# Which queue begins the attention's stores: SyncE or ScalarE

## The chip, the cores and the metric

The kernel runs on one core of a Trainium2 chip. A core has a TensorE (PE, matmuls; PEld is its weight loads), a VectorE (DVE), a ScalarE (ACT), a GpSimd (POOL) and a SyncE (SP), each with an instruction queue of its own that is worked off in order, and they wait for one another through semaphores. Transfers between DRAM and the core's memory are begun by an instruction in the queue of SP or of ACT and are carried out by 16 DMA engines. The metric is device time in microseconds (us) of one execution; lower is better.

## What is computed

A linear recurrence with a complex, input-dependent gate, per batch and head, and a gated feed-forward block behind it. Sizes: batch 4, heads 8, sequence 768, head dimension 48, model width 384, inner width 1024.

```python
for t in range(S):                      # S_re, S_im: 48 x 48 per batch and head
    new_re = ar * S_re - ai * S_im      # ar, ai: the gate at t, its size capped at 0.999
    new_im = ar * S_im + ai * S_re
    S_re, S_im = new_re + k[t] v[t]^T, new_im
    y[t] = q[t] S_re
x = y as (batch, seq, 384)
h = gelu(x @ w_in);  u, v = halves of h
v_n = layernorm(v) * g_ln
v_s[t] = sum over s of w_sg[t, s] * v_n[s] + b_sg[t]
out = x + (u * v_s) @ w_out
```

## The kernel before

The recurrence is worked as attention in chunks of 128 positions: 4 batches of 6 chunks, numbered 0 to 23. The gates' logarithms and phases are summed along the sequence, `q` and `k` are turned by them into `Q` and `K` (two rows of 48 per head), and for each chunk the masked products `am` and the state `S` of the chunk before are multiplied with `V` and `Q` into `py`, in PSUM. From batch 1 on, the turned `q` and `k` go through DRAM (`rq`, `rk`) and come back as `Q` and `K` in the layout that the matmuls want.

The step at issue is the end of `attend(g)`, chunk by chunk. `py` is copied into the tile `yp` (128 partitions x 512 floats) by ACT, or, where the order carries a mark, by DVE. `yp` has one buffer. Then two DMAs, one for the even and one for the odd heads, store it into the DRAM buffer `xd[b][j]`, which holds the attention's result of 256 positions, two chunks. That makes 24 chunks x 2 = 48 stores of 96 KB. The feed-forward part begins with `load_x`, which reads `xd[b][j]` back, transposed by the way it was laid out, from SP's queue; it is read a second time for the residual. `normal` computes the normed half, `expand` the other, `spatial` the mix over positions and the output product.

The order of all work is written out by hand. Each step of the kernel is a Python generator, and the string `ORDER` names which one goes on next: `a2` is the attention of chunk 2, `z` loads or makes `K` and `Q`, `g`, `e`, `p`, `s` and `t` are the gates' functions, `w` prepares weights, `n`, `x` and `y` are the feed-forward parts, `v` and `l` are loads, `h` and `k` check the inputs' range. `a0:2` takes two steps, a prime moves a copy from ACT to DVE (or an elementwise operation to POOL or DVE). The program order on each engine is the order in which the tokens emit instructions for it. The copy into `yp` is one step of `attend`, and the two stores are the next. In some chunks the two follow each other directly, as for chunk 15 (`a15:2`); mostly other tokens stand between them. Chunk 2's copy is the last `a2` of line 39 and its stores the `a2` of line 40:

```python
n0:5 a3 z4 g5 z4:6 z5 m4 a2 e3 v4 m4 e4 a4 v5 a3 p4 z4 e4' e4 e4' p4 z5 a4:3 z5 e3 z5' a4 p4 s4:3 a3 n1 n0 e4 g5 n0
```

Between the two, `z4` has ACT copy three tiles of `K` and `Q`, and `g5` and others run on it. On ACT's queue the stores' place is therefore behind those. Chunk 5's stores stand behind a copy of `dec` (`e4`), chunk 11's behind `vh` (`n4` and `n3`), chunk 12's behind the logarithm of a gate unit (`g10`), chunk 16's ahead of `x7`. SP's queue holds nearly all other DMAs in the same order: the loads of gates, `q`, `k`, `v`, weights and `x`, the round trip through `rk` and `rq`, and the output's stores. Each of its instructions waits for what it reads, for the buffer that it writes, and for the DMA that used its semaphore before. Only the last three stores of the output are begun by ACT.

Of the kernel before, what the change touches and what calls it, by code (L numbers as in the profile page):

```python
# [75 lines left out]
def tile_kernel(ctx: ExitStack, tc: tile.TileContext, t_q, t_k, t_re, t_im, u_q, u_k, u_re, u_im, v, q, k, f_re, f_im,  # L76
                w_in, g_ln, w_sg, b_sg, w_out, out):
    nc = tc.nc


    B, S, H, D = v.shape
# [112 lines left out]
    def ew():  # L194

        return nc.gpsimd if alt[0] == 1 else nc.vector

    def evac(out, in_):
        if alt[0]:
            nc.vector.tensor_copy(out, in_)  # L200
        else:
            nc.scalar.copy(out, in_)  # L202
# [101 lines left out]
    def fea(n):  # L304
        return units[n][0] > 0
# [247 lines left out]
    def attend(g):  # L553
        n, i = at_chunk[g]
        b, c = divmod(g, NCH)
        u = U[n]
        V = vbuf[g % 2]
        K, Q = (lambda h, nm=nm: u[nm, i, h // 4][:, h % 4, :] for nm in "KQ")
        last = c == NCH - 1
        if not last and not fea(n):  # L560
            kh = lambda h: u["k0", i][:, h].rearrange("p a d -> p (a d)")
        elif not last:
            kh = lambda h: kt_[:, h]
            kt_ = ap_.tile([P, H, 2 * D], F32, tag="kt", name="kt", bufs=2)
            for g2 in range(2):
                pk = pst.tile([P, 4, 2 * D], F32, tag="t", name="pk")
                for hh in range(4):
                    nc.tensor.transpose(pk[:, hh, :], K(4 * g2 + hh), ident[0:2 * D, 0:2 * D])  # L568
                yield
                evac(kt_[:, 4 * g2:4 * g2 + 4, :], pk)  # L570
                yield
        ams = []
        for g2 in range(2):
            pa = pst.tile([P, 4, P], F32, tag="t", name="pa")
            for hh in range(4):
                h = 4 * g2 + hh
                nc.tensor.matmul(pa[:, hh, :], K(h), Q(h), start=True, stop=True)  # L577
            yield
            am = ap_.tile([P, 4, P], F32, tag="am", name="am", bufs=2)
            nc.vector.tensor_tensor(out=am, in0=pa, in1=mask.unsqueeze(1).broadcast_to([P, 4, P]), op=ALU.mult)  # L580
            ams.append(am)
            yield
        Sb = run.get(("S", g - 1))
        if not last:
            ps = pst.tile([2 * D, H, D], F32, tag="t", name="ps")
            for h in range(H):
                nc.tensor.matmul(ps[:, h, :], kh(h), V[:, h * D:(h + 1) * D], start=True, stop=True)  # L587
            yield
            Sn = ap_.tile([2 * D, H, D], F32, tag="S", name="S", bufs=2)
            if c == 0:  # L590
                by = u["dec"][:, i, :].unsqueeze(2).broadcast_to([2 * D, H, D])
                nc.vector.tensor_tensor(out=Sn, in0=ps, in1=by, op=ALU.mult)
            else:
                nc.vector.tensor_tensor(out=Sn, in0=ps, in1=Sb, op=ALU.add)
                yield
                by = u["dec"][:, i, :].unsqueeze(2).broadcast_to([2 * D, H, D])
                ew().tensor_tensor(out=Sn, in0=Sn, in1=by, op=ALU.mult)
            run["S", g] = Sn
            yield
        py = pst.tile([P, NP, P], F32, tag="t", name="py")  # L600
        for p_ in range(NP):
            for e in range(2):
                h = 2 * p_ + e
                nc.tensor.matmul(py[64 * e:64 * e + 64, p_, :], V[:, h * D:h * D + 64], ams[h // 4][:, h % 4, :],  # L604
                                 start=True, stop=c == 0)
            if c > 0:
                for e in range(2):
                    h = 2 * p_ + e
                    nc.tensor.matmul(py[64 * e:64 * e + D, p_, :], Sb[:, h, :], Q(h),  # L609
                                     start=False, stop=True)  # L610
        yield
        yp = ap_.tile([P, NP, P], F32, tag="yp", name="yp", bufs=1)
        evac(yp, py)
        yield
        j, r = divmod(c, UC)
        dst = xd[b][j].rearrange("(p e d) t -> e d p t", e=2, d=D)[:, :, :, r * P:(r + 1) * P]
        for e in range(2):
            nc.sync.dma_start(out=dst[e], in_=yp[64 * e:64 * e + D])
        yield


# [266 lines left out]
    for g in range(B * NCH):  # L888
        chains.update({f"v{g}": load_v(g), f"r{g}": rotate(g), f"z{g}": heads(g), f"a{g}": attend(g)})
# [59 lines left out]
```

## Time and profile before

| | us |
|---|---|
| median of 2 runs | 462.36 (460.3 and 464.41) |
| the profiled execution | 457.97 |
| its span, first to last instruction | 456.3 |
| PE idle within the span | 35.6 |
| SP: waits of the stores for a copy by ACT, 10 of them | 25.2 |
| SP: waits of `x` loads for the stores, 6 of them | 12.5 |
| ACT: waits of a `yp` copy for the stores before it, 2 of them | 7.4 |

How to read the profile's lines. A line of a timeline gives the start in us, the length in us, engine, source line, operation, what is written and read, shapes, count, and in brackets the idle time of the engine just before it with what ended it. SPq and ACTq are instructions of a queue that keep its engine's datapath idle: issues of DMAs and waits. A line of the table of windows gives the stretch in us, its length, busy time of PE, PEld, DVE, ACT and POOL with the number of instructions, the TensorE clock granted, the DMA engines' share and the GB/s moved. A view of one tile lists its instructions with minimum, median and maximum length in ns. In the chain of waits a row is a start, a length and what the end of the program waited for in that stretch; a DMA there is its way from the issue to the landing. The page's rows of DMA queues give packets, MB and share.

### The profile page before, as it was taken

Reading aid. Unit: us, or ns where it says so; the run is one execution under the profiler, and the core shown is the slowest. Engines: PE = TensorE matmul, PEld = TensorE weight load, DVE = VectorE, ACT = ScalarE, POOL = GpSimd, SP = SyncE. Lnnn points to the kernel's source line nnn. Section 1 sums busy time; section 2 is a strip of 40 time slices with the busy share of each in tenths; the row PEclk is TensorE's granted clock in tenths of the full one; section 3 lists DMA queues with packets and bytes.
Section 4 is the critical chain, followed back from the end, with each engine's and each line's share of the span. In section 5 each row is a group of like instructions: output and inputs, shape, how many; then the busy total and the mean of one; then the engine's idle time right before and its main releaser. Section 6 shows DMA issues by size and latency. Waiting matters only on the chain.

```text
span 456.3 us, 9462 instructions
## 1 busy us (share of the span) xinstructions
PE 420.7 (92%) x3658; PEld 388.5 (85%) x3658; DVE 372.1 (82%) x646; ACT 284.9 (62%) x383; POOL 170.6 (37%) x208
## 2 busy tenths in 40 slices
PE   1568898899999999999999999999999999999994
PEld 0255697788999999999999989998999989989994
DVE  4999999899899989998886897679797637875643
ACT  6899999698969999958568546675540312321000
POOL 7036223726446385143233528632314303423000
PEclk9999999999999999999999999999999999999999
DMA  7688675667766787876857696695688684625321
GB/s 224 228 246 253 209 214 130 207 184 244 210 185 212 254 256 232 252 234 203 227 161 270 170 349 203 206 290 193 185 241 265 209 245 145 178 71 185 106 70 42
DMA packets 67710, 93.40 MB, mean 205 GB/s; under 512 B 9540, under 2 KB 52550, under 8 KB 67656
## 3 DMA queue, kind: packets, MB, share of 16 engines
q1 hardware_dynamic: 67224, 92.32, 66.6%
q8 instruction: 30, 0.49, 0.5%
q10 hardware_dynamic: 432, 0.39, 0.3%
q14 instruction: 24, 0.20, 0.1%
HBM read 69.09 MB, written 23.60 MB: 203 GB/s over the span
## 4 chain that ended last, share of the span: by engine, by line
PE 60%; DVE 14%; DMA 9%; ACT 7%; POOL 4%; issue 3%; SPq 2%; POOLq 0%; DVEq 0%; ACTq 0%
PE pvs L219 17%; PE pu L219 9%; PE pa L577 8%; PE po L219 7%; PE pv L219 7%; PE ps L587 4%; DMA K<-rk 3%; PE py L604 3%; PE py L609 2%; ACT L188 2%; DMA x<-xd 2%; PE pk L568 2%; DMA xd<-yp 1%; DMA raw<-in_moe_w_in_dram 1%; DVE im L367 1%
## 5 line engine op out<-in xcount | busy, mean ns | idle before, releaser
L188 ACT ACT_TABLE_LOAD x67 | 86.0, 1283 | 2.0 <-PEq L934 0.8
L219 PE MATMUL pvs<-wsgh,vh 128*128 128x256 f32 x288 | 82.4, 286 | 0.1
L219 PE MATMUL pvs<-wsgh,vl 128*128 128x256 f32 x288 | 81.1, 282 | 0.4 <-DVE vl L689 0.3
L219 PE MATMUL pvs<-wsgl,vh 128*128 128x256 f32 x288 | 80.9, 281 | 0.0
L577 PE MATMUL pa<-Q,K 96*128 96x128 f32 x384 | 49.9, 279 | 6.0 <-ACT Q L202 3.2
L219 PEld LDWEIGHTS pvs<-wsgh,vh 128*128 128x128 f32 x288 | 54.3, 189 | 0.8 <-issue 0.4
L219 PEld LDWEIGHTS pvs<-wsgh,vl 128*128 128x128 f32 x288 | 54.3, 188 | 0.8 <-DVE vl L689 0.8
L219 PEld LDWEIGHTS pvs<-wsgl,vh 128*128 128x128 f32 x288 | 54.3, 189 | 0.0
L577 PEld LDWEIGHTS pa<-Q,K 96*128 96x128 f32 x384 | 45.9, 192 | 9.7 <-ACT Q L202 4.3
L219 PE MATMUL pu<-xh,winh 128*128 128x256 f32 x144 | 42.6, 296 | 0.2 <-ACT dec L202 0.2
L219 PE MATMUL po<-gh,wouth 128*128 128x256 f32 x144 | 41.7, 290 | 0.6 <-DVE gh L211 0.6
L219 PE MATMUL po<-gl,wouth 128*128 128x256 f32 x144 | 40.8, 283 | 1.3 <-POOL gl L214 1.0
L219 PE MATMUL pu<-xh,winl 128*128 128x256 f32 x144 | 40.6, 282 | 0.0
L219 PE MATMUL pu<-xl,winh 128*128 128x256 f32 x144 | 40.5, 282 | 0.0
L219 PE MATMUL po<-gh,woutl 128*128 128x256 f32 x144 | 40.5, 282 | 0.0
L604 PE MATMUL py<-am,vbuf 128*64 128x128 f32 x384 | 36.5, 278 | 0.8 <-DVE am L580 0.8
L580 DVE TENSOR_TENSOR am<-pa,mask 128x512 f32<-128x512 f32 x48 | 31.8, 678 | 5.5 <-PE pa L577 5.4
L609 PE MATMUL py<-Q,S 96*48 96x128 f32 x320 | 31.2, 272 | 0.0
L189 ACT ACTIVATE vr<-pv 128x512 f32<-128x512 f32 x24 | 14.2, 598 | 24.6 <-PE pv L219 16.8
L219 PE MATMUL pv<-winh,xh 128*128 128x512 f32 x72 | 29.2, 406 | 0.0
L219 PEld LDWEIGHTS po<-gl,wouth 128*128 128x128 f32 x144 | 27.2, 189 | 1.9 <-POOL gl L214 1.2
L219 PEld LDWEIGHTS po<-gh,wouth 128*128 128x128 f32 x144 | 27.1, 188 | 1.5 <-DVE gh L211 0.8
(287 smaller groups left out, 1144.7 us busy)
## 6 DMA issues: line engine op xcount, KB each, us to landing
x<-xd SPq DMA_DIRECT2D x24, 384.0 KB, 4.7
K<-rk SPq DMA_DIRECT2D x18, 384.0 KB, 5.7
Q<-rq SPq DMA_DIRECT2D x18, 384.0 KB, 5.0
vbuf<-in_v_dram SPq DMA_DIRECT2D x24, 192.0 KB, 3.7
xd<-yp SPq DMA_DIRECT2D x48, 96.0 KB, 3.5
gr<-in_f_re_dram SPq DMA_DIRECT2D x12, 384.0 KB, 3.6
gr<-in_f_im_dram SPq DMA_DIRECT2D x12, 384.0 KB, 3.4
re<-in_u_re_dram SPq DMA_DIRECT2D x9, 384.0 KB, 5.4
```

What stands on the lines that cost most here:

```text
L188: nc.scalar.preload_act_table_set(SETS[t])
L189: nc.scalar.activation(out, in_, func, scale=scale, **kw)
L219: nc.tensor.matmul(o, w(i), x(i), start=(i == 0 and j == 0), stop=(i == n - 1 and j == 2))
L367: ew().tensor_mul(im, im, e)
L568: nc.tensor.transpose(pk[:, hh, :], K(4 * g2 + hh), ident[0:2 * D, 0:2 * D])
L577: nc.tensor.matmul(pa[:, hh, :], K(h), Q(h), start=True, stop=True)
L580: nc.vector.tensor_tensor(out=am, in0=pa, in1=mask.unsqueeze(1).broadcast_to([P, 4, P]), op=ALU.mult)
L587: nc.tensor.matmul(ps[:, h, :], kh(h), V[:, h * D:(h + 1) * D], start=True, stop=True)
L604: nc.tensor.matmul(py[64 * e:64 * e + 64, p_, :], V[:, h * D:h * D + 64], ams[h // 4][:, h % 4, :], start=True, stop=c == 0)
L609: nc.tensor.matmul(py[64 * e:64 * e + D, p_, :], Sb[:, h, :], Q(h), start=False, stop=True)
```

## The change

The two stores of each chunk are begun from ACT's queue instead of SP's. They keep their place in the hand-written order, so they stand on ACT behind whatever ACT instructions come before the stores' token. Data, shapes and the `yp` buffer stay as they were.

```diff
         j, r = divmod(c, UC)
         dst = xd[b][j].rearrange("(p e d) t -> e d p t", e=2, d=D)[:, :, :, r * P:(r + 1) * P]
         for e in range(2):
-            nc.sync.dma_start(out=dst[e], in_=yp[64 * e:64 * e + D])
+            nc.scalar.dma_start(out=dst[e], in_=yp[64 * e:64 * e + D])
         yield
```

## The prediction

> **What bounds the kernel now.** I read the page first, then the table of windows, then the view of the tile `yp`, then the timelines of SyncE's queue (SP), ScalarE (ACT) and TensorE (PE) where PE stands idle, and last the chain of waits. The page:
>
> ```profile
> span 456.3 us, 9462 instructions
> PE 420.7 (92%) x3658; PEld 388.5 (85%) x3658; DVE 372.1 (82%) x646; ACT 284.9 (62%) x383; POOL 170.6 (37%) x208
> q10 hardware_dynamic: 432, 0.39, 0.3%
> ```
>
> PE is busy for 420.7 us of 456.3. A gain can only come out of the 35.6 us in which it isn't, most of them before the first store starts at 41.2 us. A loss comes wherever PE's next operand is late. ACT's 62% is a mean over unlike stages, so the table of windows (PE, PEld, DVE, ACT, POOL):
>
> ```profile
> 30.00:60.00 30.00, 25.37 (x198) 19.50 (x198) 29.19 (x52) 28.63 (x45) 11.48 (x9) 1.00 0.80 238
> 75.00:90.00 15.00, 11.83 (x116) 10.51 (x113) 13.88 (x24) 11.26 (x19) 9.80 (x8) 1.00 0.71 202
> 90.00:105.00 15.00, 13.84 (x117) 12.36 (x118) 13.22 (x21) 14.88 (x19) 5.00 (x5) 1.00 0.75 216
> 125.00:218.00 93.00, 93.00 (x854) 88.91 (x853) 87.03 (x131) 79.03 (x97) 43.45 (x41) 1.00 0.75 229
> ```
>
> Up to 105 us ACT is nearly full and PE has holes; from 125 to 218 PE has none, ACT is at 85%. The stores, from the view of `yp`, and the only DMAs that ACT issues today:
>
> ```profile
> L618 SPq DMA_DIRECT2D xd<-yp x48: 303/434/1279, 41.2 to 390.1; - x48
> L200 DVE COPY yp<-py x5: 676/681/692, 120.0 to 327.2; 128x512 f32<-128x512 f32 x5
> DMA to landing us min/median/max: 1.9/3.5/6.4
> L753 ACTq DMA_DIRECT2D out_dram<-x x3: 338/381/912, 449.7 to 451.9; - x3
> ```
>
> So 24 pairs, each two issues of 0.434 us in the median, landing 3.5 us after the issue. `yp` has one buffer: the next copy waits until the pair before it has landed. PE's four places that the change can reach:
>
> ```profile
> 78.97 1.16 PE L577 MATMUL pa<-Q,K 96*128 96x128 f32 x8 [1.27 <-ACT Q L202]
> 103.17 0.44 PE L568 MATMUL pk<-ident,K 96*128 96x96 f32 x3 [1.13 <-DMA K<-rk]
> 225.74 0.47 PE L568 MATMUL pk<-ident,K 96*128 96x96 f32 x3 [0.51 <-ACT yp L202]
> 373.22 0.47 PE L568 MATMUL pk<-ident,K 96*128 96x96 f32 x3 [1.05 <-DMA K<-rk]
> ```
>
> The brackets hold PE's idle time and what ended it: one copy on ACT, two K loads that stand behind stores on SP, one `yp` copy that waited for a landing. Together they are 3.96 us.
>
> **The change part by part.** Removed: 48 issues from SP, 48 x 0.434 = 20.8 us, and SP's waits for `yp` ahead of them. Added: the same 20.8 us and waits to ACT's queue, at the place of the store's token in the hand-written order, which is often several ACT instructions after the copy's token. Nothing else is reordered, and the bytes are the same. What counts is where each pair stands on ACT against where it stood on SP.
>
> *Chunk 2, about 76 us, the largest term.*
>
> ```profile
> 72.69 0.88 SPq L618 DMA_DIRECT2D xd<-yp  x2
> 77.72 1.57 SPq L618 DMA_DIRECT2D xd<-yp  x2
> 81.22 0.38 SPq L640 DMA_DIRECT2D x<-xd  x1
> 94.81 0.81 SPq L618 DMA_DIRECT2D xd<-yp  x2
> 96.65 0.43 SPq L548 DMA_DIRECT2D K<-rk  x1
> ...
> 75.89 0.59 ACT L202 COPY K<-pk 96x512 f32<-96x512 f32 x1
> 76.37 0.86 ACT L189 ACTIVATE em<-l 128x768 f32<-128x768 f32 x1
> 77.11 0.58 ACT L202 COPY yp<-py 128x512 f32<-128x512 f32 x1
> 78.32 0.59 ACT L202 COPY Q<-pk 96x512 f32<-96x512 f32 x1
> 95.74 1.28 ACT L188 ACT_TABLE_LOAD   x1
> ```
>
> By the order the pair of chunk 2 stands between the `K` copy of 75.89 and the `em` of 76.37. SP issued it at 72.69. On ACT the first issue can begin once the `K` copy is under way, about 75.97, the second at 76.4, and 3.5 us later, at 79.9, it has landed. The `yp` copy of chunk 3, now at 77.11, waits for that: 79.9 - 77.11 = 2.8 us. Behind it on ACT stand the `Q` copy of 78.32, for which PE waits at 78.97 with no slack, and the exponentials of that unit. So 2.8 us on the path. Bounds by the same view's 1.9 and 6.4: 1.2 to 5.7.
>
> *Chunk 5, 95 us, and the K load.* SP stood at the pair of 94.81 until `yp` was copied, and the K load of 96.65, for which PE waits at 103.17, was queued behind it. With the pair gone from SP, K waits only for what it reads and for its buffer, and PE's hole of 1.13 us closes: -1.1 (bounds -1.13 to 0, the latter if `rk`, itself later by the term before, is then what ends last). On ACT the pair comes before the table load of 95.74, behind a short copy that covers little: ACT is later by up to 0.8, in a window where it is busy 14.88 of 15 us. I take 0.4 (0 to 0.8).
>
> *Chunks 9 and 8, 166 to 172 us.*
>
> ```profile
> 166.47 0.94 ACT L189 ACTIVATE inv<-l,cols 128x768 f32<-128x768 f32 x1
> ...
> 169.69 0.59 ACT L202 COPY yp<-py 128x512 f32<-128x512 f32 x1
> 172.04 0.60 ACT L189 ACTIVATE vr<-pv 128x512 f32<-128x512 f32 x1 [0.46 <-PE pv L219]
> ```
>
> Chunk 9's pair stands behind the `inv` of 166.47; its second issue is at 166.95 at the earliest and lands at 170.45, 0.8 after the `yp` copy of 169.69 wants to start. Chunk 8's pair stands directly behind that copy and is bare, 0.87. Less the 0.46 of slack, the `vr` of 172.04 is 1.2 late. PE has other work queued there; I take 0.5 (0 to 1.2).
>
> *Chunk 11, 197 us.*
>
> ```profile
> 192.88 0.80 SPq L618 DMA_DIRECT2D xd<-yp  x2
> 196.86 0.38 SPq L640 DMA_DIRECT2D x<-xd  x1
> 196.66 0.73 ACT L189 ACTIVATE vh<-vr,ny 128x512 fp32r<-128x512 f32 x1
> 201.84 0.84 ACT L189 ACTIVATE xh<-x 128x768 fp32r<-128x768 f32 x1 [1.47 <-PE pu L219]
> ```
>
> The pair comes behind the `vh` of 196.66, and SP's load of `x`, which reads what it stores, goes from 196.86 to about 197.1 + 3.5 = 200.6, with six loads queued behind it. That is 3.7 us on a load whose reader, `xh`, has 1.47 us of idle time ahead of it. I take 0.6 (0 to 2.2).
>
> *Chunk 12, 219 us.*
>
> ```profile
> 218.19 0.99 SPq L618 DMA_DIRECT2D xd<-yp  x2
> 218.62 6.42 DMA xd<-yp
> 219.37 0.94 ACT L189 ACTIVATE l<-l,cols 128x768 f32<-128x768 f32 x1
> 225.10 0.58 ACT L202 COPY yp<-py 128x512 f32<-128x512 f32 x1 [4.80 <-DMA xd<-yp]
> ```
>
> Here the landing itself is on the path: 6.42 us after the issue, behind three loads on the same queue, then the `yp` copy, then PE at 225.74. ACT reaches the pair while it runs the `l` of 219.37, so the second issue goes from 218.62 to 219.8, 1.2 later. If the landing takes as long as now, that is +1.2; if it no longer stands behind the three loads, the hole of 0.51 closes. I take +0.6 (-0.5 to 1.2).
>
> *Chunk 20, 364 us.*
>
> ```profile
> 363.69 0.87 SPq L618 DMA_DIRECT2D xd<-yp  x2
> 365.60 0.48 SPq L548 DMA_DIRECT2D K<-rk  x1
> ```
>
> SP issues from the pair to the K load without a break; take out 0.87 and K goes that much earlier, against a hole of 1.05 us at 373.22. But the stores' bytes travel at the same time all the same: -0.6 (-1.05 to 0).
>
> *The rest.* Chunks 0 and 1 fall in the window where ACT is busy 28.63 of 30 us: +0.4 (0 to 2 x 0.87 = 1.7). The other pairs I cost at nothing: they are covered by the ACT instruction before them or by an idle stretch behind; if that cover is gone, each costs ACT 0.87. Five copies are made by DVE, and there ACT now waits for DVE. The longest such wait is chunk 16's:
>
> ```profile
> 294.86 0.81 SPq L618 DMA_DIRECT2D xd<-yp  x2
> 296.09 0.60 ACT L189 ACTIVATE u__3690<-pu 128x512 f32<-128x512 f32 x1 [2.87 <-PE pu L219]
> ```
>
> By the order its pair stands on ACT ahead of a table load and this gelu. ACT is held from about 292 until 294.86 + 0.87 = 295.7, the table load (1.28) ends at 297.0, and the gelu is 0.9 late. PE wants its buffer only some matmuls later: 0 (0 to 0.9). The program's DMAs also take turns on eight semaphores, and each issue waits for the DMA eight before it; at the pairs' places on ACT that one has landed, but for chunk 15, where ACT has a long idle stretch behind the pair: 0.
>
> The sum: 2.8 - 1.1 + 0.4 + 0.5 + 0.6 + 0.6 - 0.6 + 0.4 = 3.6 us, between -1.5 and 13.8 when all ends are added. The profiled execution took 457.97 us, of which 456.3 are its span; 457.97 + 3.6 = 461.6. It is 4.4 us under the median of the two runs shown, 462.36, and on that scale, on which I predict, it is 466.0.
>
> How long an issue holds ACT is the open price. The row of 77.72 shows a pair of 1.57 us on SP against 0.88 for that of 72.69. [...] No run here shows both queues issuing at once.
>
> **The rivals.**
>
> *ACT becomes the bound.* Nothing in the trace shows a DMA issue beside ACT's own work: the three that it has run at the end, when it is idle. If nothing covers an issue, the pairs up to 105 us, six of them, cost 6 x 0.87 = 5.2 instead of the parts of them counted above, and the six that ACT would issue from 125 to 218 us, at 85% ACT, as much again; with the late landing of chunk 2 and the K load's gain, 5.2 + 5.2 + 2.8 - 1.1 = 12.1 us: 474.5. For it: ACT's 14.88 of 15 us. Against it: PE's work ahead in the 93 us without a hole. It decides if the pairs from 125 on cost more than about 0.4 us of PE each.
>
> *Faster: SP was the queue that hurt.* If a store no longer queues behind loads, chunk 2's pair lands soon enough that the `Q` copy is not late, and the holes at 103.17, 225.74 and 373.22 close: -1.13 - 0.51 - 1.05 = -2.7 us, 459.7. For it: 6.42 us of landing at 218.62 against 1.9 for the fastest. Against it: even 1.9 us lands chunk 2 at 78.3, after 77.11. It decides if ACT starts that pair before about 75.2 us, that is, if its queue runs ahead of its engine. [...]
>
> *The change does nothing that shows.* Every late pair is taken up by PE's work ahead: -0.5 to +0.5, 462.4. Against it: the 78.97 row has no slack.
>
> **How the numbers follow.** Two per cent is 9.2 us, about what a measurement of this kernel can tell from no change. The forecast, +1 to +9 us, gets 0.5; no visible effect 0.14; the faster rival 0.15, nearly all of it within 2%; ACT as the bound 0.21, of which 0.17 is over 2%. Faster by over 2% would need PE to lose 9.2 us of holes where the stores reach 3.96: 0.04. So slower 0.18, same 0.78, faster 0.04. The range goes from the faster rival less 1.7 for the spread of the runs shown, 458, to the end of the ACT rival, 474.
>
> **What would show it.** The line of the stores appears under ACT's queue with 48 issues and no longer under SP's; the second DMA queue goes from 432 packets and 0.39 MB to about 5.1 MB (48 x 96 KB more). PE's wait for the `Q` copy near 79 us grows from 1.27 to about 4 us, with ACT's `yp` copy before it held by a landing. The hole at 103 us is gone or small; the `x` load near 197 us starts 3 to 4 us later. The prediction is wrong if the `yp` copy near 77 us does not wait, if the pairs' issues on ACT take much over 0.43 us each, or if PE shows new holes between 125 and 218 us.

## The result, and the profile after

| | before | after |
|---|---|---|
| median of two runs, us | 462.36 (460.3 to 464.41) | 477.12 (475.3 to 478.94) |
| profiled execution: time and span, us | 457.97 and 456.3 | 475.3 and 473.6 |
| its mean granted clock of TensorE | 0.998 | 0.978 |

The changed kernel takes 1.0339 times as long, with a 95% interval of 1.0277 to 1.0401: slower by 14.8 us. The forecast was 466.0, with a range of 458 to 474, and no difference that can be measured as the likeliest class. Both were wrong.

From the page of the kernel after: the span, the engines' busy times, the granted clock in 40 slices, the two DMA queues (packets, MB, share of the engines) and the chain that ended last, by engine.

```profile
span 473.6 us, 9463 instructions
PE 430.4 (91%) x3658; PEld 396.6 (84%) x3658; DVE 370.6 (78%) x646; ACT 285.2 (60%) x383; POOL 168.4 (36%) x208
PEclk9999999697999999999999999998999999999999
q1 hardware_dynamic: 57240, 87.60, 60.3%
q10 hardware_dynamic: 10416, 5.12, 4.0%
PE 55%; DMA 16%; DVE 15%; ACT 8%; POOL 3%; issue 2%; SPq 0%; ACTq 0%; DVEq 0%; POOLq 0%
```

ACT is busy for 285.2 us, where it was 284.9: the issues did not fill it. PE is busy for 9.7 us longer with the same 3658 instructions, and the row of its clock, all nines before, has dips. So time went in two ways: PE stood idle longer, and behind that it ran slower. The view of the tile `yp`:

```profile
L618 ACTq DMA_DIRECT2D xd<-yp x48: 309/404/1213, 41.2 to 407.4; - x48
  ACT yp L202: 19.8, 4
  DVE yp L200: 4.5, 2
DMA to landing us min/median/max: 1.9/4.6/9.9
```

An issue costs 0.404 us in the median, not more than the 0.434 on SP. But the pairs now land 4.6 us after the issue instead of 3.5, at most 9.9 instead of 6.4, and copies on ACT wait 19.8 us for such landings, those on DVE 4.5. (The trace tells the landing of 24 of the 48 stores before and of 36 after, so the two medians are not of the same stores; the waits are of all copies.)

Where the time is lost shows best against PE's own progress. Take the end of the last matmul into `py` (L604, L609) of the 2nd, 6th, 8th, 12th, 16th, 18th and 22nd chunk in PE's order, and the time from each to the next; in the kernel before these ends lie at 49.79, 93.54, 121.42, 189.24, 252.59, 290.24 and 362.56 us. All of it is worked out from the timelines of the profiled executions:

```
stretch of before, us   0-50   50-94  94-121 121-189 189-253 253-290 290-363 363-end
before                 49.79   43.75   27.87   67.83   63.34   37.65   72.33   93.70
after                  49.63   49.03   34.39   68.09   64.75   37.52   76.80   93.38
after less before      -0.16   +5.28   +6.52   +0.26   +1.41   -0.13   +4.47   -0.32
```

The sum is +17.3, the difference of the spans, and 16.3 of it lies in three stretches. Each has one place, and the timelines of the kernel after show it (start, duration, engine, line, operation; in brackets the idle time ahead and what ended it).

```profile
75.91 0.46 ACTq L618 DMA_DIRECT2D xd<-yp  x1
80.44 0.59 ACT L202 COPY yp<-py 128x512 f32<-128x512 f32 x1 [3.18 <-DMA xd<-yp]
81.67 0.57 ACT L202 COPY Q<-pk 96x512 f32<-96x512 f32 x1
82.29 1.01 PE L577 MATMUL pa<-Q,K 96*128 96x128 f32 x3 [4.67 <-ACT Q L202]
...
96.18 0.33 SPq L548 DMA_DIRECT2D K<-rk  x1
96.56 0.75 SPq L329 DMA_DIRECT2D k<-in_u_k_dram  x1
98.87 0.33 SPq L548 DMA_DIRECT2D Q<-rq  x1
99.29 0.38 SPq L548 DMA_DIRECT2D K<-rk  x1
99.92 0.81 ACTq L618 DMA_DIRECT2D xd<-yp  x2
110.23 0.59 ACT L202 COPY yp<-py 128x512 f32<-128x512 f32 x1 [6.76 <-DMA xd<-yp]
111.36 0.58 PE L219 MATMUL pu<-xh,winh 128*128 128x256 f32 x1 [5.28 <-ACT vr L189]
```

First place: chunk 2's pair, issued at 75.91, lands just before 80.44; chunk 3's copy has waited 3.18 us for it, `Q` stands behind the copy, and PE has stood for 4.67 us. Second place: chunk 5's pair of 99.92 lands at about 110.2, the next copy has held ACT for 6.76 us, and PE has stood for 5.28. In the kernel before, SP issued `k`, `Q`, `K` and `q` behind that pair, within 2.4 us (its timeline; the `K` of 96.65 stands between the last two); now four such loads go in the 4 us ahead of it.

```profile
95.67 0.46 SPq L329 DMA_DIRECT2D k<-in_u_k_dram  x1
96.23 0.37 SPq L548 DMA_DIRECT2D Q<-rq  x1
97.12 0.43 SPq L329 DMA_DIRECT2D q<-in_u_q_dram  x1
```

The third place, from the chain of waits of the kernel after (start, duration, what):

```profile
304.59 5.30 DMA xd<-yp
310.01 0.70 DVE yp L200
```

And from its timelines of ACT and PE:

```profile
304.24 0.81 ACTq L618 DMA_DIRECT2D xd<-yp  x2
310.74 0.81 ACTq L618 DMA_DIRECT2D xd<-yp  x2
311.57 1.28 ACT L188 ACT_TABLE_LOAD   x1 [6.69 <-DVE x L751]
312.87 0.60 ACT L189 ACTIVATE u__3690<-pu 128x512 f32<-128x512 f32 x1
319.27 0.46 ACT L202 COPY kt<-pk 128x384 f32<-128x384 f32 x1
319.78 2.08 PE L577 MATMUL pa<-Q,K 96*128 96x128 f32 x8 [2.39 <-ACT kt L202]
```

Chunk 17's pair of 304.24 has landed at 309.89. Only then may DVE make chunk 16's copy, and chunk 16's pair stands on ACT's queue until that copy is done, so ACT does nothing for 6.69 us. From 311.57 on it works with a single pause of 0.20 us until `kt` is copied, and PE has stood for 2.39 us waiting for `kt`. In the timeline of the kernel before, the same `kt` is this one:

```profile
302.50 0.45 ACT L202 COPY kt<-pk 128x384 f32<-128x384 f32 x1
```

It starts 12.26 us after the mark at 290.24; in the kernel after, 15.86 us after the mark at 303.41. The gelu `u__3690`, the second instruction behind the hold, is late by the same 3.6 us. (From 310.01 on the chain of waits takes another way, through a load of `x` that lands at 318.38 and an instruction `gr` of ACT. But that `gr` began at 318.36, directly behind the work ahead of it on ACT; the hold on ACT explains its time.)

What the holes do to the clock, from the table of windows of the kernel after (PE, PEld, DVE, ACT, POOL busy; then the granted clock):

```profile
78.00:82.00 4.00, 0.00 (x0) 0.00 (x0) 1.01 (x3) 1.56 (x3) 1.14 (x1) 0.86 0.28 45
82.00:86.00 4.00, 3.71 (x19) 3.67 (x20) 2.87 (x6) 3.48 (x5) 2.72 (x3) 0.50 0.00 0
86.00:90.00 4.00, 4.00 (x33) 3.90 (x34) 3.86 (x8) 3.02 (x4) 1.95 (x4) 0.50 0.28 54
90.00:94.00 4.00, 4.00 (x38) 3.68 (x35) 3.22 (x4) 0.58 (x1) 0.00 (x0) 0.86 0.65 205
```

After 4.67 us without a matmul PE works at half its clock until about 91 us. The same happens near 112 (0.63) and 321 (0.50).

### The profile page after: what moved, and what is told of

It reads as the page before. It is cut to its first block, busy times and chain, and to the rows that moved or that the text cites. A ratio compares the mean times of both kernels' runs of the same rounds, so it can differ in the third digit from the quotient of the medians.

```text
span 473.6 us, 9463 instructions
## 1 busy us (share of the span) xinstructions
PE 430.4 (91%) x3658; PEld 396.6 (84%) x3658; DVE 370.6 (78%) x646; ACT 285.2 (60%) x383; POOL 168.4 (36%) x208
## 3 DMA queue, kind: packets, MB, share of 16 engines
q10 hardware_dynamic: 10416, 5.12, 4.0%
## 4 chain that ended last, share of the span: by engine, by line
PE 55%; DMA 16%; DVE 15%; ACT 8%; POOL 3%; issue 2%; SPq 0%; ACTq 0%; DVEq 0%; POOLq 0%
PE pvs L219 16%; PE pu L219 8%; DMA xd<-yp 8%; PE pa L577 7%; PE po L219 6%; PE pv L219 6%; PE ps L587 4%; PE py L604 3%; DMA x<-xd 2%; PE py L609 2%; ACT L188 2%; DMA wr<-in_moe_w_in_dram 1%; DMA raw<-in_moe_w_in_dram 1%; PE pk L568 1%; DVE im L367 1%
## 5 line engine op out<-in xcount | busy, mean ns | idle before, releaser
L577 PE MATMUL pa<-Q,K 96*128 96x128 f32 x384 | 52.1, 287 | 8.9 <-ACT Q L202 4.7
L577 PEld LDWEIGHTS pa<-Q,K 96*128 96x128 f32 x384 | 48.1, 199 | 12.8 <-ACT Q L202 5.6
L604 PE MATMUL py<-am,vbuf 128*64 128x128 f32 x384 | 37.7, 285 | 1.5 <-DVE am L580 1.5
L219 PEld LDWEIGHTS pu<-xh,winh 128*128 128x128 f32 x144 | 27.6, 191 | 7.0 <-ACT vr L189 5.5
L609 PE MATMUL py<-Q,S 96*48 96x128 f32 x320 | 32.1, 279 | 0.0
L202 ACT COPY yp<-py 128x512 f32<-128x512 f32 x19 | 11.0, 579 | 32.0 <-DMA xd<-yp 19.8
```

Source lines behind the costliest of these rows:

```text
L219: nc.tensor.matmul(o, w(i), x(i), start=(i == 0 and j == 0), stop=(i == n - 1 and j == 2))
```

## The experiments

Four theories were to be told apart. A: `yp` has one buffer, so a pair that lands late holds the next copy and all that stands behind it on its engine. B: the pairs land later because SP's loads no longer queue behind them. C: the issues themselves cost ACT. D: the clock that falls behind a hole is a loss of its own. Two words on the expectations below: a unit's two chunks don't always come in order of their numbers, so the 5th pair in time is chunk 5's and the 17th chunk 17's, and where an expectation speaks of the pairs or landings of "chunks 4 and 16" it counts them in time from 0; the edits name the code's own numbers.

**Five pairs back on SP.**

```diff
-            nc.scalar.dma_start(out=dst[e], in_=yp[64 * e:64 * e + D])
+            (nc.sync if g in (2, 5, 12, 16, 17) else nc.scalar).dma_start(out=dst[e], in_=yp[64 * e:64 * e + D])
```

> The kernel after, with the pairs of chunks 2, 5, 12, 16 and 17 begun from SP again, 19 pairs still from ACT. A with D: the holes near 82, 111, 239 and 320 are gone, the clock is 0.99 or more, and the time is 460 to 464. C: 19/24 of the 14.8 us stay, about 474.

Measured: 461.35 us, 1.0034 of before (0.9989 to 1.0079). Nineteen pairs from ACT cost nothing that can be measured, by the interval at most 0.8%: C does not make the 14.8 us, and all of the loss that can be measured sits in these five.

**Only chunks 2 and 5 from ACT**, the other way round.

```diff
-            nc.sync.dma_start(out=dst[e], in_=yp[64 * e:64 * e + D])
+            (nc.scalar if g in (2, 5) else nc.sync).dma_start(out=dst[e], in_=yp[64 * e:64 * e + D])
```

> The kernel before, with only the pairs of chunks 2 and 5 begun from ACT. If the loss comes from single late landings (A) and from the clock that falls behind the long holes they make (D), two pairs of 24 carry over half of it: PE idle 4 to 5 us near 80 and near 110, the granted clock under 0.7 behind each, and 469 to 474. If the loss is spread over all issues (C): 24/2 less, about +1 us, 463 to 464.

Measured: 470.72 us, 1.0196 (1.0111 to 1.0281). By the time, two pairs of 24 carry more than half of the loss. The profiled execution is less clear: 4.42 us more than before lie in 50-94 and 3.86 in 94-121, about half of the 17.3, but another 5.23 lie in 0-50, where neither pair is.

**A second buffer for every other chunk, on ACT and on SP.** There is no room for a second `yp`; the buffer of `tg`, of the same size, is lent.

```diff
-        yp = ap_.tile([P, NP, P], F32, tag="yp", name="yp", bufs=1)
+        yp = (mp.tile([P, NP, P], F32, tag="tg", name="yp") if g % 2 == (g < 8) else
+              ap_.tile([P, NP, P], F32, tag="yp", name="yp", bufs=1))
```

> The kernel after, with a second buffer for `yp` (chunks take turns between its own and the one of `tg`, of the same size). Theory A, one buffer: a late store only hurts because the next copy, and all that stands behind it on its engine, waits for its landing; then the 19.8 us (ACT) and 4.5 us (DVE) of copies waiting for a landing go to under 4 together, PE's holes of 4.67 (82 us), 1.35 (239) and most of the 5.28 (111) go, the clock keeps near 1.00, and the time is 462 to 467. Theory C, the issues themselves fill ACT: the second buffer changes nothing for ACT's occupation, and the time stays at 473 or more. Theory B, loads no longer held behind the stores take the DMA engines: the landings stay long (median over 4 us) here too, and what then waits for them is the load of x; 466 to 472.

> The kernel before (all stores on SP), with the same second buffer: the control for the run with two buffers on ACT. Theory A: before lost only 7.4 (ACT) and 0.8 us (DVE) to such waits, of which PE felt the 0.51 near 226 and the 1.27 near 79 in part, so 460 to 463. Theories B and C say nothing else here.

Measured: 470.24 us, 1.0195 (1.0109 to 1.0281), on ACT, and 469.98 us, 1.0244 (1.0152 to 1.0337), on SP. No copy waits for a landing any more in the first, but the control on SP, where 460 to 463 was expected, is as slow: the lent buffer has a cost, since copies and the users of `tg` now wait for each other (in the view of `yp` one copy's engine idles for 13.1 us until `tg` is read, and for 13.6 us in the control). With that, the pair of runs says nothing about the queues except that both come out alike. It can't decide on A; the next one lends the buffer only at four places, where little else uses `tg`.

**A second buffer at four places only**, on ACT, and its control on SP.

```diff
-        yp = ap_.tile([P, NP, P], F32, tag="yp", name="yp", bufs=1)
+        yp = (mp.tile([P, NP, P], F32, tag="tg", name="yp") if g in (3, 5, 12, 17) else
+              ap_.tile([P, NP, P], F32, tag="yp", name="yp", bufs=1))
```

> The kernel after, with a second buffer for `yp` at four places only (chunks 3, 5, 12 and 17 use that of `tg`, at times when little else uses it; with all chunks taking turns the sharing itself cost 10 us, on SP as on ACT). Theory A (one buffer): the copies no longer wait for the landings of chunks 2, 4, 12 and 16; the holes near 82, 239 and 320 go back to what they were, the one near 111 to under 3 us, no window of the clock at 0.50 is left but perhaps one near 111, and the time is 461 to 467. If something else holds ACT at these places, the holes stay and the time is 474 or more.

> The control to the run with four second buffers on ACT: the kernel before, all pairs on SP, with the same four second buffers. Theory A says that with these buffers it no longer matters which queue begins the stores: this one gains only the 0.51 us near 226 and perhaps part of 7.4 us of waits on ACT, 458.5 to 461, a ratio to before of 0.995 to 1.00, and not more than 0.5 per cent under that run's 0.9999. If the buffers had given ACT's version back with one hand what the issues on ACT cost with the other (theory C), this one is 1 per cent or more under before.

Measured: on ACT 460.47 us, 0.9999 of before (0.9960 to 1.0039); on SP 457.17 us, 0.9922 (0.9885 to 0.9958). The view of `yp` of the kernel on ACT:

```profile
L619 ACTq DMA_DIRECT2D xd<-yp x48: 309/356/1857, 42.6 to 393.0; - x48
  ACT yp L202: 3.7, 1
  DVE yp L200: 1.2, 1
DMA to landing us min/median/max: 1.9/3.9/7.4
```

All 48 issues are on ACT, and against the kernel before the whole 3.4% is gone, with the waits of copies at 3.7 and 1.2 us. That is theory A. The control is faster than had been expected of it, and than either kernel: before, too, lost some 3 us to the one buffer, in 189-253 and 253-290 (63.34 and 37.65 us there, 62.14 and 35.77 in the control). So with the same four buffers ACT's queue still stands some 0.8% behind SP's, more than the 0.5% that had been allowed to A, each measured against its own runs of before, with intervals that all but touch. The one buffer thus makes about 2.6 of the 3.4%. Where the other 3 us are stays open, and the issues themselves (C) are not excluded for them.

**The second buffer at one place at a time.** The same edit with `g in (3,)`, `(5,)` and `(12, 17)`:

> The kernel after, with a second buffer for chunk 3's `yp` alone, so that its copy no longer waits for chunk 2's pair. The whole set of four gave back 15.8 us. The hole near 82 falls from 4.67 to 1.3 and the clock stays at 1.00, but the 1.89 near 90 comes back: 3.4 + 4.4 - 1.9 = 5.9 less, 471. If the first term of the predicted sum, 2.8 us, was right in size: 474.3.

> The kernel after, with a second buffer for chunk 5's `yp` alone, so that the next copy (chunk 4's, near 110) no longer waits for chunk 5's pair of 99.9 us. The hole of 5.28 near 111 falls to under 2, with 1.8 us of slow clock: 5 to 6 less, 471 to 472. If the landing, not the copy that waits for it, sets the end there (through the load of x near 115): 475 or more.

> The kernel after, with a second buffer for the `yp` of chunks 12 and 17 alone. The holes of 1.35 near 239 and 2.39 near 320, with 1.2 us of slow clock behind the latter, go: 4 to 5 less, 472 to 473. If the 4.5 us that DVE's copies wait there are covered by PE's work ahead, as the prediction had it for chunk 16: 475.5 or more.

Measured: 469.87 us, 1.0187 (1.0135 to 1.0239); 472.55 us, 1.0274 (1.0231 to 1.0317); 467.89 us, 1.0124 (1.0076 to 1.0172). The first two are near what had been expected, though that of chunk 5 alone is not clear of the kernel after (1.0277 to 1.0401) by its time; the third is 4 us faster than expected. The stretches, worked out as above, show that each buffer repairs its own place; the two other places move by up to 1.9 us from one execution to another:

```
stretch of before, us   0-50   50-94  94-121 121-189 189-253 253-290 290-363 363-end
before                 49.79   43.75   27.87   67.83   63.34   37.65   72.33   93.70
after                  49.63   49.03   34.39   68.09   64.75   37.52   76.80   93.38
buffer at 3            49.31   45.13   33.03   68.09   63.54   38.60   78.25   93.60
buffer at 5            50.76   47.18   28.62   68.29   64.04   37.20   76.52   92.63
buffer at 12, 17       52.31   47.42   34.44   68.01   63.42   35.77   72.34   93.04
buffer at all four     51.91   45.68   27.68   68.71   62.98   36.09   72.34   93.94
SP held (below)        49.58   48.16   27.86   68.14   64.27   38.40   78.07   92.48
behind copy (below)    51.99   46.98   33.91   71.08   62.83   35.77   74.50   92.65
matmuls, 1st (below)   49.14   47.02   35.44   67.43   65.71   38.01   76.46   92.90
```

Chunk 3's buffer brings 50-94 from 49.03 to 45.13, chunk 5's brings 94-121 from 34.39 to 28.62, those of 12 and 17 bring 290-363 from 76.80 to 72.34 and besides take what before lost in 253-290. The first column wanders from 49 to 52 us between executions, and was 55.0 in the run with only chunks 2 and 5 on ACT, where every pair of that stretch is on SP: so it need not come from the change.

**The pair directly behind its copy.** The code waits one step of the written order between copy and pair; without that step the pair is issued at once.

```diff
         evac(yp, py)
-        yield
         j, r = divmod(c, UC)
```

> The kernel after, with the pair issued in the order directly behind its copy instead of at its later token. If its late place on ACT is what makes a pair late (theory A, place), chunk 2's pair goes at about 71.4 instead of 75.5 and has landed before chunk 3's copy wants to start at 77.1: the hole near 82 falls from 4.67 to about 1.3 us and the clock stays at 1.00 behind it (another 4.4 us); chunk 12's pair goes 5 us earlier and the hole near 239 closes. The pairs of chunks 4 and 16 already stood directly behind their copies, so the holes near 111 and 320 stay. In all 8 to 9 us less than after: about 468. If it is the landing itself that is long on ACT's queue wherever the pair stands (theory B alone): 474 or more.

Measured: 471.12 us, 1.0250 (1.0185 to 1.0315). Half right. In this trace chunk 2's pair has landed before the next copy, and 189-253 loses nothing any more; but 50-94 is still 3.2 us over before, with a hole of 2.25 us near 84 where 1.3 had been expected. And a pair directly behind its copy is bare. In the timeline of ACT:

```profile
74.00 0.58 ACT L202 COPY yp<-py 128x512 f32<-128x512 f32 x1
74.61 0.81 ACTq L617 DMA_DIRECT2D xd<-yp  x2
75.46 1.08 ACT L189 ACTIVATE vr<-pv 128x512 f32<-128x512 f32 x2 [0.88 <-ACT yp L202]
```

ACT stands for 0.88 us while its queue waits for the copy and issues twice, where in the kernel after the issues of 75.51 and 75.91 run beside the copy of 75.81. 121-189, where ACT is at 85%, is 3 us longer for it. In these two traces an issue is free on ACT only behind work that is still running.

**SP held as before.** A transfer of 16 bytes out of `yp`, where SP's store stood, makes SP's later loads wait for the copy again; the stores stay on ACT.

```diff
             nc.scalar.dma_start(out=dst[e], in_=yp[64 * e:64 * e + D])
+        nc.sync.dma_start(out=tiny, in_=yp[0:1, 0, 0:4])
```

> The kernel after, with a transfer of 16 bytes out of `yp` on SP where the store's token stands (into a scratch tile that nobody reads), so that SP's later loads are held until `yp` is copied, as they were before, while the stores stay on ACT. Theory B (loads that no longer stand behind the stores take the DMA engines from them): the landings of the pairs of chunks 0, 4, 16 and 20, 5.1, 10.2, 5.7 and 5.8 us after, go back to 2.7, about 5, 2.7 and 4.3, the holes near 111 and 320 go, and the time is 463 to 468, the hole near 82 being the place that stays. If the landings are long for another reason, or only the place counts: they stay, and the time is 476 to 479.

Measured: 470.18 us, 1.0233 (1.0166 to 1.0300), between the two forecasts. It tells two kinds of late landing apart. Near 100 the holding cures it: the copy behind chunk 5's pair waits 0.65 us instead of 6.76, and 94-121 is back at 27.86.

```profile
103.20 0.59 ACT L202 COPY yp<-py 128x512 f32<-128x512 f32 x1 [0.65 <-DMA xd<-yp]
```

There the loads ahead of the pair were the cause. The start times of the DMA packets in the traces show how: in the kernel after, the first of the pair's 416 packets passes at 104.37, 4.45 us after the issue, and 1.14 MB of SP's pass in between, nearly three loads of 384 KB; with SP held the first passes 0.82 us after the issue. Being on a DMA queue of its own, q10, did not let the pair pass the loads that SP had issued before it on q1.

In 290-363 the holding cures nothing (78.07). There the loads are issued behind the pair as in the run with five pairs on SP, and the pair is on q10 instead of q1 (what also differs: the pair's second half, at 297.59, is issued beside SP's first load). First that run, with the pair on SP:

```profile
294.10 0.82 SPq L618 DMA_DIRECT2D xd<-yp  x2
294.96 0.46 SPq L334 DMA_DIRECT2D vbuf<-in_v_dram  x1
295.46 0.43 SPq L346 DMA_DIRECT2D gr<-in_f_re_dram  x1
297.30 0.69 DVE L200 COPY yp<-py 128x512 f32<-128x512 f32 x1 [0.91 <-DMA xd<-yp]
```

And SP held, with the pair on ACT:

```profile
297.24 1.08 ACTq L619 DMA_DIRECT2D xd<-yp  x2
297.53 0.35 SPq L335 DMA_DIRECT2D vbuf<-in_v_dram  x1
298.00 0.37 SPq L347 DMA_DIRECT2D gr<-in_f_re_dram  x1
302.99 0.69 DVE L200 COPY yp<-py 128x512 f32<-128x512 f32 x1 [3.46 <-DMA xd<-yp]
```

The next copy can start 3.2 us after the pair on SP and 5.75 after the pair on ACT, although the loads come behind its first half both times. What went between, from the DMA view of the kernel after in 303 to 311 us (packets, MB, share of the engines' time):

```profile
q1 hardware_dynamic: 1099, 2.21, 90.6%
q10 hardware_dynamic: 416, 0.20, 9.6%
```

The pair's 416 packets are of 0.5 KB in the mean, SP's 1099 of 2 KB. Per DMA engine (16) that is 26 against 69, and one of SP's takes 0.906 x 8 us / 69 = 0.105 us. While the pair's 416 packets pass, from 305.51 to 309.06 us in the kernel after, SP's queue passes 422, and 452 in the run with SP held, about one for one. That gives an estimate: 26 of SP's packets on each engine while the pair's pass are 26 x 0.105 = 2.7 us, close to the difference of 2.55. No run shows what sets this share, and it does not explain chunk 5's pair, of which no packet passed for 4.45 us.

**Matmuls in the holes.** Extra matmuls (ident on ident, overwritten at once) keep PE busy where it stood idle, without making anything come earlier. 30 and 40 of them in the first two holes, 14 and 18, and at last 22 in the first alone:

```diff
             pa = pst.tile([P, 4, P], F32, tag="t", name="pa")
+            for _ in range(22 if (g, g2) == (4, 0) else 0):
+                nc.tensor.matmul(pa[:, 0, :], ident, ident, start=True, stop=True)
```

> The kernel after, with 30 and 40 more matmuls (ident on ident, into tiles that are overwritten right behind) in front of the holes of 4.67 us near 82 and of 5.28 us near 111: about 3.6 and 4.8 us more work for PE, in time in which it stood idle. Theory D (a hole of over about 2 us halves the clock for 3 to 11 us, and that is a loss of its own): the holes fall to about 1 us, the clock behind them stays at 1.00, and although PE does more work the time falls by the 4.4 and 1.8 us that the slow stretches cost, to about 471. If the low clock has another cause, or costs nothing: 477 to 479.

> As the run with 30 and 40 extra matmuls, which took twice the time meant (0.23 us each, 6.8 and 9.0 us), filled both holes wholly and ended 0.8 us behind them: now 14 and 18, about 3.2 and 4.1 us. Theory D: the holes near 82 and 111 fall from 4.67 and 5.28 to 1.2 to 1.5 us, the clock behind them stays at 1.00, and the time falls by most of the 4.4 and 1.8 us, to 471 to 473, with 7.3 us more work on PE than in the kernel after. If the clock costs nothing: 477 or more.

> The kernel after, with 22 extra matmuls (ident on ident, overwritten at once, 5.0 us) in the hole of 4.67 us near 82 alone. Theory D (the halved clock behind a hole is a loss of its own that reaches the end): the hole falls under 1 us, the clock stays at 1.00 from 82 to 104, PE is at the transposes that it reached at 104.2 us about 3 us sooner, and the time is 472 to 474.5. If what the slow clock costs there is taken up by holes that it closes later (the 1.89 us near 90 that the kernel before has and after has not): 476 to 478.

Measured: 474.21 us, 1.0300 (1.0249 to 1.0351); 475.39 us, 1.0331 (1.0289 to 1.0374); 474.60 us, 1.0319 (1.0283 to 1.0356). The first overfilled the second hole (PE worked on filler until 112 us, behind the hole's old end); the second left 1.86 us of the first hole, and the clock fell all the same. The third is the clean one. The table of windows, that run first:

```profile
75.00:90.00 15.00, 14.98 (x150) 14.49 (x150) 11.86 (x21) 9.25 (x14) 8.86 (x8) 1.00 0.39 90
```

And the kernel after:

```profile
75.00:90.00 15.00, 10.31 (x71) 9.53 (x70) 10.60 (x20) 10.31 (x15) 6.48 (x8) 0.69 0.32 71
```

The clock stays at 1.00, and 50-94 falls by 2.0 us, from 49.03 to 47.02, with 5 us more work on PE. That fits D, at half the size expected: about 2 of the 5.28 us lost there would be the clock's. It is one execution against another, and the size is not settled: the run with 30 and 40 matmuls took 46.69 us there, but four others that keep the hole and the slow clock took 47.18 (buffer at 5), 47.42 (buffer at 12, 17), 48.16 (SP held) and 48.17 (only chunks 2 and 5 on ACT). The rest of its slow work would be taken up by the hole of 1.89 us near 90, which before has and after has not. That the time of the whole kernel fell the runs can't say: the interval of this ratio overlaps that of the kernel after.

**The buffers and a few matmuls together**, 5 and 7 of them ahead of the holes near 80 and 91:

```diff
+            for _ in range({(4, 0): 5, (5, 0): 7}.get((g, g2), 0)):
+                nc.tensor.matmul(pa[:, 0, :], ident, ident, start=True, stop=True)
```

> All pairs from ACT, the four second buffers, and 5 and 7 extra matmuls (ident on ident, overwritten at once) ahead of the two holes of 1.33 and 1.89 us that are left near 80 and 91. A hole of 1.88 or 1.89 us halved the clock in two of six traces and not in the four others. Theory D: with the holes filled the clock cannot fall there, the slowest runs go and the median is 457 to 460, 0 to 3 us under before. If holes under 2 us cost only themselves, and filling them only moves the idle time into useless work: 460 to 461, the same as with the buffers alone.

Measured: 458.95 us, 0.9959 (0.9929 to 0.9990), within the expected 457 to 460, against 0.9999 (0.9960 to 1.0039) with the buffers alone: the intervals overlap, so the gain of the filler is not shown, and the longest run, 466.41 us, is longer than the longest with the buffers alone, 462.12. The fastest kernel of all is the one that moves nothing to ACT and lends four buffers.

## Why the prediction was wrong

Its sum, put into the same stretches, stands against what was measured:

```
stretch of before, us   0-50   50-94  94-121 121-189 189-253 253-290 290-363 363-end   sum
predicted               +0.4    +2.8    -0.7    +0.5    +1.2     0       0      -0.6    3.6
measured               -0.16   +5.28   +6.52   +0.26   +1.41   -0.13   +4.47   -0.32   17.3
```

Two slips of the sums change nothing: its upper ends add up to 13.7, not 13.8, and the end of the ACT rival, 474.5, stands as 474 in the range.

*Right.* 48 issues went to ACT, the second queue has 5.12 MB. Chunk 3's copy waited, 3.18 us for 2.8, and PE's hole came to 4.67 where "about 4" was said. The hole near 103 closed. Issues are mostly covered by the instruction ahead of them, 0.404 us each in the median and 19.6 us for all 48, against 21.9 on SP. PE has no new hole from 125 to 218. The stretches of the pairs near 166 to 172, 197, 219 and 364 came out within 0.3 us of what was given, less than they differ between executions, so that this tests no single term.

*Wrong by 7.2 us: chunk 5 and the K load.* The step saw only that SP, free of the pair, would bring K sooner, and counted a gain. It did; but it left the pair's landing as it was. Set free, SP issued four loads in the 4 us ahead of the pair, the pair took 9.9 us, the next copy waited, and all of ACT behind it. The question put to chunk 2, who waits for a landing of up to 6.4 us, was not put to this pair at all.

*Wrong by 4.5 us: chunks 17 and 16, near 291.* Chunk 17's pair was among those of "The other pairs I cost at nothing", because its issue is covered. It is, but a covered issue is not a landing on time: the next copy could start 3.08 us after that pair in the kernel before and 5.77 after it in the kernel after. For chunk 16 the prediction had the mechanism, ACT held until DVE has copied, but priced it with the old landing: the gelu 0.9 us late, and 0 for PE, which would have work ahead. The gelu was 3.6 us late, everything behind it on ACT with it, and it was `kt`, not the gelu, for which PE then stood 2.39 us, with a window of slow clock behind.

*Wrong by 2.5 us: chunk 2.* Mechanism, place and hole were right, the copy's wait in part by luck: the second issue came 0.5 us sooner than predicted, 75.91 for 76.4, and the landing took 4.5 us for 3.5. What was missing is the clock behind the hole, about 2 us if the run with the filled hole has its size right. The granted clock was 0.50 from 82 to 90 us. The profile of before shows no such fall behind its holes from 36 to 440 us, the longest of 1.89 us; the runs show one behind each of the 15 holes of 2.7 to 5.8 us, so that a hole of "about 4 us" costs more than its length.

In one sentence: the prediction took the issue for the price of a store, and carried the landing of the old queue over to the new.

*The rivals.* "ACT becomes the bound" gave 474.5, near to the time, for the wrong reason: ACT is as busy as before, 19 pairs lose nothing that can be measured, and 24 with four buffers 0.8% against SP with the same buffers. "Faster: SP was the queue that hurt" had landings from ACT's queue shorter; they are longer, 4.6 us for 3.5 in the median. Chunk 17's pair took longer on q10, beside SP's longer packets on q1, than on q1 ahead of them: 5.75 us to the next copy with SP held, 3.2 with the pair on SP. Chunk 5's pair waited until the loads issued before it had passed: 1.14 MB of SP's in the 4.45 us ahead of its first packet.

## What to carry to other kernels

Before moving a DMA to another queue, ask who waits for its landing and for its source buffer, and what it stood ahead of: in the kernel before, SP issued four loads within 2.4 us behind chunk 5's pair; with SP set free it issued four in the 4 us ahead of it, and the pair took 9.9 us to land. Where a buffer has no spare, a later landing is an engine's wait, and a second buffer at the few places that bind (here four chunks of 24) can be worth more than the choice of the queue (here about 2.6 of the 3.4%). On the queue of an engine that computes, an issue that waits for another engine holds its own engine too (here ACT for 6.69 us). Count a hole in PE of about 2 us or more together with the slow clock behind it: 30 of the 38 holes of 1.85 to 5.8 us had one.

## What the runs showed of the hardware

In the 17 profiled executions, from 36 to 440 us, each of the 15 holes of 2.7 to 5.8 us in PE's work had windows at about half the clock within 4 us of its end, 15 of the 23 holes of 1.85 to 2.4 us had, and 1 of the 50 of 0.85 to 1.84.

The clock records of the traces show more. In the kernel after the clock goes to 0.50 at 80.84, 108.15 and 319.78 us, for 10.24, 6.83 and 3.41 us, and stands at 1.00 for 17.07 and 204.80 us between: all multiples of 3.41 us. In each of the traces its changes lie on such a grid, and the 31 slow stretches are one, two or three windows of 3.41 us long (15, 9 and 7 of them). In the kernel after PE was idle for 94, 61 and 70% of the three windows ahead of the falls. In all traces the 25 windows at full clock of which PE was idle for more than half were followed by one at 0.50, 6 of the 32 that were idle for 34 to 49% were, and none of the 1317 that were idle for less. So in these traces the place of a hole on the grid counted as well as its length: a hole of 2.39 us near 320 fills 70% of one window in the kernel after, and the clock falls; one of 2.40 in the run with chunk 5's buffer alone fills at most 45% of any, and it stays.

The hole near 90 that before has, 1.89 us long, stands in six other executions with 1.87 to 1.90 us. In four of these the clock is at 0.50 to 0.56 in a stretch of 2 us behind it; in before and the two others it stays at 1.00. That may be a part of the spread between runs of one kernel; it was not tried.
